# A two-layer attention and MLP kernel: bf16 residual, two-row shift instructions on GpSimd, more plane buffers and another rule table

## The chip, the cores and the metric

The kernel runs on one core of a Trainium2 chip. The metric is the device time of one launch in microseconds; three runs of the kernel before gave 1496.22, 1497.7 and 1498.02 us, a median of 1497.7 us. A profiled execution of the same kernel gives the trace from which all views below come.

The core has five engines with a queue of instructions each: TensorE (PE; its weight loads are shown apart as PEld), VectorE (DVE), ScalarE (ACT), GpSimd (POOL) and SyncE (SP, which only starts DMAs). Each works through its queue in order and waits on semaphores for the others.

## The reference

Two kinds of layer, A and B, are applied in turn, twice, to x of 2048 positions by 512 channels, each on the layer-normed residual stream:

```python
def _A_ref(x, wq, wk, wv, wo):          # H = 32 heads of 16, one key and value head
    q = (x @ wq) split into heads
    k = x @ wk
    v = x @ wv
    scores = einsum("bhqd,bkd->bhqk", q, k) * (Dh ** -0.5)
    p = softmax(scores)
    return (p @ v, heads joined) @ wo

def _B_ref(x, w1, w2, w3, w4):          # w1, w2: 512x512; w3: 512x1792; w4: 1792x512
    h = gelu(layernorm(x) @ w1)
    hs = (four quarters of h, shifted by 1, -1, 2, -2 positions) @ w2
    x1 = x + hs
    return x1 + gelu(layernorm(x1) @ w3) @ w4

x = x + A(layernorm(x)); x = x + B(layernorm(x)); x = x + A(layernorm(x)); x = x + B(layernorm(x))
```

The softmax over 32 x 2048 x 2048 scores, twice, is by far the largest part: 268 million exponentials.

## The kernel before

**Halves.** A layer's attention is worked through in chunks of 512 queries (the last 512 of the second layer as two chunks of 256), each in 8 blocks of four heads, each over 16 tiles of 128 keys. One *half* is one key tile of 512 queries for two of the four heads (at 256 queries two key tiles), so a layer has 1024 halves and the kernel 2048. `make_groups` lists them in order. A half needs two score matmuls (`qk`, L1079), 1024 exponentials in each of 128 partitions, and matmuls P·V (`declare_pv`, L1203) that add into one PSUM bank, ACC, with a 17th column of ones for the softmax denominator.

**Two ways to the exponential.** A half is either a *unit* (`declare_unit`): ScalarE reads two score banks and writes EA (L1123), and one P·V of four matmuls takes it. Or it is a *pair* (`declare_pair`): VectorE turns each score bank into the bit pattern of a bf16 number by one multiply and add into 16-bit integers, the plane J (two instructions of 128x512, L1144). That is a power of two with a straight line between powers, and to lessen its error two copies shifted by 43 and by 85 (a third and two thirds of the 128 steps of an exponent) are made, the planes JK (L1154, 128x1024 each), and P·V runs three times, on J and both JK, with value matrices VD scaled by `PARTS`. The shifts go to GpSimd while fewer than `ADDS` of them are pending there, else to VectorE.

**The rest.** After a block, `block_end` copies ACC, forms reciprocals and normalises. After a chunk, `chunk_end` declares the output projection (L1423 adds it to the residual X), and the MLP: `mixer_in` (layer norm, w1, GELU of GP on ScalarE, L1466), `mix` (w2, L1504), `mlp` (layer norm, w3, evictions G by L1541, GELU of G by L1546), `mlp_out` (w4, L1567 adds to X, or L1572 writes the output), and `next_kv` (layer norm, keys and values of the next layer). GELU and exponential need different ScalarE tables, so each change between them is a table load. The residual X is float32 (X32), with the bf16 input in the upper halves of the same rows (X16).

**The layer boundary.** Halves of the second layer's first chunk need keys of all positions, but their first blocks may run early on the keys that exist: 7 blocks over key tiles 0 to 5, then over tiles 6 to 10 (`EARLY`), with the partial sums spilled to SBUF. So 1024 + 84 = 1108 halves can be done before keys of tiles 6 to 10 are there.

**The order.** `Plan` is a list scheduler that runs when the program is built: it keeps a model of the engines, takes the ready operation of the best priority, and emits a fixed order for each engine. `assign` decides when a half becomes a pair. A table of rules (`MOODS`), chosen anew for each stretch of 12.5 us of planned time by a character of `TEMPER`, sets its thresholds. Where TensorE would be idle, `filler` adds matmuls of zeros (ONES, NIL). Three PSUM banks are shared by pairs and all MLP work; units have four of their own in two slots.

Of the kernel before, what the change touches and what calls it, by code (L numbers as in the profile page):

```python
# [8 lines left out]
dt = mybir.dt  # L9
# [6 lines left out]
class Late:  # L16


    __slots__ = ("bank", "ops", "gates")

    def __init__(self):
        self.bank = None
        self.ops = []
        self.gates = []


class Op:
    __slots__ = ("eng", "emit", "preds", "npend", "succ", "dur", "prio", "seq", "ready", "start",
                 "end", "take", "give", "dma", "out", "pos", "sem", "vc", "side", "placed", "pe", "feeds", "port", "parts", "after", "entry")


class Plan:
# [170 lines left out]
    def _pick(self, eng, t, dense=False):  # L203
# [15 lines left out]
        for o in h:  # L219
            if o.ready > t + 1e-9 or o.entry > t + self.EAGER:  # L220
                continue
            if eng == "ACT" and self.closing and o.side and not all(u.placed for u in self.units[-4:]):
                continue
            if joins and (o.pe[0] != self.pe_kind or self.begin(o, t) > t + 1e-9):
                continue
            if limit and o.prio > 0:
                end = self.run_end(o, t)
                if (not joins or end > self.pe_end + 0.02) and \
                        any(end + (self.SWITCH if o.pe[0] != "Q" else 0.0) > x for x in limit):
                    continue  # L230
            if pressing and self.run_end(o, t) > self.pe_end + 0.02:
                continue
            key = (low.get(o, o.prio), o.seq)
            if self.CLOSE and eng == "PE" and o.prio > 2 and o not in low and o.take is None:
                key = (self.CLOSE, o.seq)
            if stick and o.prio > 2 and o.pe[0] == self.pe_kind and not any(self.run_end(o, t) + self.SWITCH > x for x in due):
                key = (self.STICK, o.seq)
            if o in pinned:
                key = (self.PINNED, o.seq)
            if best is not None and key > best[0]:  # L240
                continue
            k = None
            if o.take is not None:
                if not all(p.placed and (p.end <= t + 1e-9 or p.eng == "PE") for p in o.take.gates):
                    continue
                margin = self.MARGIN if o.side else self.LAT["PE"]
                for i, (ft, b) in enumerate(self.pool):
                    if ft + margin <= t + 1e-9 and (k is None or ft < self.pool[k][0]):
                        k = i
                if k is None or o.prio > 2 and len(self.pool) <= self.SPARE and self.attach is not None and not self.loose:  # L250
                    continue
            best = (key, o)
            bank = k
# [4 lines left out]
        if o.take is not None:  # L258
            b = self.pool.pop(bank)[1]
            o.take.bank = b  # L260
            last = self.pool_last.get(b)
            if last is not None:
                o.preds.add(last)
# [63 lines left out]
    def _place(self, o, t):  # L327
# [51 lines left out]
        if o.give is not None:  # L379
            self.pool.append((o.end, o.give.bank))  # L380
            self.pool_last[o.give.bank] = o
            heapq.heappush(self.events, o.end + self.LAT["PE"])
            heapq.heappush(self.events, o.end + self.MARGIN)
# [146 lines left out]
class Kernel:  # L530
# [12 lines left out]
    N_EA = 6  # L543
    N_J = 4
    N_JK = 5
    STEPS = (0, 43, 85)
    ADDS = 4
    PARTS = (0.3203125, 0.25390625, 0.2021484375)
# [8 lines left out]
    AHEAD = 2  # L557
    MAX_PAIRS = 2
# [27 lines left out]
    TEMPER = "0004c7ec07f77e4f907027ef07eeee79fc406e0770e7473e37722cc100f0b580559f773c3777120e4e54ee2fe471e1217c7e4070c38e21c731"  # L586
# [25 lines left out]
    def memory(self):  # L612
        self.sbytes = 0
        sb = self.sb
        x32 = self.stack.enter_context(self.nc.sbuf_tensor("X32", [128, 16 * 512], dt.float32))[:, :]
        self.sbytes += 32768
        self.X32 = self.shaped(x32, [16, 512])
        self.X16 = self.shaped(x32.bitcast(dt.bfloat16), [16, 1024])[:, :, 512:1024]
# [27 lines left out]
        self.J = sb("J", [self.N_J, 1024], dt.uint16)  # L646
        self.JK = sb("JK", [self.N_JK, 1024], dt.uint16)
        spare = self.JK[:, 0, :].bitcast(dt.bfloat16)
        self.G2E = [(self.EA[:, f // 2, f % 2, :], ("EA", f // 2)) for f in range(2 * self.N_EA)]
        self.G2E += [(spare[:, f * 512:(f + 1) * 512], ("JK", 0)) for f in range(14 - 2 * self.N_EA)]  # L650
# [59 lines left out]
    def head(self):  # L710
# [9 lines left out]
        def load_x(c):  # L720
            for h in range(2):
                t0 = c * 4 + h * 2
                load(self.X16[:, t0:t0 + 2, :], xin[:, t0:t0 + 2, :],
                     [("X", t0), ("X", t0 + 1)], 2 * 131072, c)
# [161 lines left out]
    def ln_in(self, la, tiles, prio=None):  # L886
# [3 lines left out]
        src = (lambda tb: self.X16[:, tb, :]) if la == 0 else (lambda tb: self.X32[:, tb, :])  # L890
        base = (self.QS, "QS") if la and tiles[0] > 2 else (self.ZR, "ZR")
        slot = self.slot(la, c)
        for part in self.portions(tiles):
            self.stats(src, part, lambda tb: ("X", tb), prio)
            self.rstd(part, prio)
            for tb in part:
                self.apply(base[0][:, tb % 4, :], src(tb), tb, [("X", tb)], [(base[1], tb % 4)],
                           0.456 if la else 0.355, prio)
# [120 lines left out]
    def make_groups(self):  # L1019
# [25 lines left out]
        for g in gs:  # L1045
            if g[5]:
                self.segs.append(dict(at=g[0:3], end=None, left=0, held=[], open=False))
            seg = self.segs[-1]
            seg["end"] = g[6]
            for p in range(2):  # L1050
                seg["left"] += 1
                self.halves.append(g[0:5] + (p, len(self.segs) - 1, g[5]))
        self.hi = 0
# [6 lines left out]
        self.waiting = []  # L1060
        self.nfill = 0
# [67 lines left out]
    def declare_pair(self, g):  # L1129

# [4 lines left out]
        js = m % self.N_J  # L1137
        J = self.J[:, js, :]
        for i in range(2):
# [5 lines left out]
                out=J[:, i * 512:(i + 1) * 512], in0=self.PB[:, L.bank, :],  # L1145
                scalar1=128 * LOG2E * 0.25, scalar2=float(127 * 128), op0=ALU.mult, op1=ALU.add),
                writes=[L, ("J", js, i)], dur=t_ps(512), prio=1, side=False, give=L)
        jt = [("J", js, 0), ("J", js, 1)]
        es = [(J, jt)]
        for k in (1, 2):  # L1150
            r = (2 * m + k - 1) % self.N_JK
            self.adds = [p for p in self.adds if not p.placed]
            eng = "POOL" if len(self.adds) < self.ADDS else "DVE"
            x = op(eng, lambda e, k=k, r=r: e.tensor_scalar(  # L1154
                out=self.JK[:, r, :], in0=J, scalar1=float(self.STEPS[k]), scalar2=1.0, op0=ALU.add,
                op1=ALU.mult),
               reads=jt, writes=[("JK", r)], dur=t_x4(1024) if eng == "DVE" else 1.12, prio=2, side=False, port=True,
                   after=0.0 if eng == "DVE" else 0.07)
            if eng == "DVE":
                o = x  # L1160
            else:
                self.adds.append(x)
            es.append((self.JK[:, r, :], [("JK", r)]))
        self.pairs.append(o)
        self.add_pv(g, [(self.shaped(ap.bitcast(dt.bfloat16), [2, 512]), tg, k, m) for k, (ap, tg) in enumerate(es)])

    def add_pv(self, g, es):
        self.segs[g[6]]["held"].append((g, es))
        while True:
            seg = self.segs[self.seg]  # L1170
            held, seg["held"] = seg["held"], []
            for g, es in held:
                if es[0][2] is None or seg["open"]:
                    for x in es:
                        self.declare_pv(seg, g, *x[:3])
                    seg["left"] -= 1
                    if es[0][2] is not None:
                        self.waiting.remove(es[0][3])
                else:
                    seg["held"].append((g, es))  # L1180
# [164 lines left out]
    def assign(self, now, p):  # L1345
# [12 lines left out]
        if self.pl.backlog() > y or \  # L1358
                self.waiting and self.ndve - self.waiting[0] >= min(self.N_J, self.N_JK // 2):
            return False  # L1360
        d = self.hi + self.AHEAD
        while d < len(self.halves) and (self.halves[d][7] or self.halves[d][5] != p or d in self.given):
            d += 1
# [46 lines left out]
    def outproj(self, la, tb, prio=4):  # L1410
# [3 lines left out]
        for h in range(2):  # L1414
            def fpe(e, h=h):
                ins = None
                for b in (2 * h, 2 * h + 1):
# [4 lines left out]
        res = self.X16 if la == 0 else self.X32  # L1422
        op("DVE", lambda e: e.tensor_tensor(out=self.X32[:, tb, :], in0=self.PB[:, L.bank, :],  # L1423
                                            in1=res[:, tb, :], op=ALU.add),
           writes=[L, ("X", tb)], dur=t_ps(512), give=L, prio=prio)

    def mixer_in(self, la, c, tiles, tail):
# [4 lines left out]
        for part in self.portions(tiles):  # L1432
            self.stats(lambda tb: self.X32[:, tb, :], part, lambda tb: ("X", tb), None)
            self.rstd(part, None, both=True)
            for tb in part:
                self.apply(self.Y[:, tb % 6, :], self.X32[:, tb, :], tb, [("X", tb)], [("Y", tb % 6)], 0.456, None)
# [71 lines left out]
    def mlp(self, la, tiles, tail):  # L1508
# [12 lines left out]
        for tb in tiles:  # L1521
            op("POOL", lambda e, tb=tb: e.tensor_tensor(out=self.X32[:, tb, :], in0=self.Y[:, tb % 6, :],  # L1522
                                                       in1=self.X32[:, tb, :], op=ALU.add),
# [28 lines left out]
    def mlp_out(self, la, tiles, tail=False):  # L1552
        op = self.pl.op
        G = [x[0] for x in self.G2E] if tail else [self.G2[:, f, :] for f in range(14)]
        for i, tb in enumerate(tiles):
# [10 lines left out]
            if la == 0:  # L1566
                op("DVE", lambda e, tb=tb, L=L: e.tensor_tensor(  # L1567
                    out=self.X32[:, tb, :], in0=self.PB[:, L.bank, :], in1=self.X32[:, tb, :], op=ALU.add),
                   writes=[L, ("X", tb)], dur=t_ps(512), give=L)
            else:  # L1570
                ob = tb % 2
                op("DVE", lambda e, tb=tb, L=L, ob=ob: e.tensor_tensor(  # L1572
                    out=self.OUTB[:, ob, :], in0=self.PB[:, L.bank, :], in1=self.X32[:, tb, :], op=ALU.add),
# [39 lines left out]
```

The softmax here doesn't subtract the row's maximum and nothing guards it: scores larger than these inputs give would overflow.

## Time and profile before

| | |
|---|---|
| median of three runs | 1497.7 us |
| the profiled execution's span | 1495.4 us |
| exponentials on ScalarE (units) | 1433 |
| pairs on VectorE | 615 |
| shifts on GpSimd / on VectorE | 1014 / 216 |
| table loads on ScalarE | 28 |
| mean granted TensorE clock | 1.000 |

In the profile a group's row names line, engine, operation, output and inputs, then count, busy time, mean duration and the idle time ahead of it with what ended most of it. Durations of one engine can overlap: a mean of 1132 ns with 1433 of them in 1318.8 us of busy time means that a new one starts every 0.920 us. The busy time by stretches, in us from the span's start (columns: stretch, length, then busy time and count of PE, PEld, DVE, ACT, POOL, then clock, DMA share and GB/s):

```profile
0.00:736.00 736.00, 722.26 (x13517) 301.95 (x13521) 687.70 (x1223) 724.85 (x774) 630.92 (x663) 1.00 0.08 19
736.00:834.00 98.00, 96.46 (x1964) 45.91 (x1960) 68.81 (x140) 85.78 (x84) 44.49 (x53) 1.00 0.01 3
834.00:1434.00 600.00, 590.99 (x13295) 268.44 (x13290) 545.90 (x958) 599.50 (x640) 524.19 (x538) 1.00 0.04 10
1434.00:1496.00 62.00, 58.57 (x1388) 36.17 (x1380) 30.55 (x66) 19.50 (x27) 12.96 (x23) 1.00 0.07 22
```

The first stretch is the head and layer one, the second the boundary between the layers, the third layer two, the last the MLP of the last queries.

### The profile page before, as it was taken

How to read it: one execution, taken by the hardware profiler on the slowest of the kernel's cores; microseconds unless marked ns; L12 is line 12 of the kernel's file. 1: busy time of each engine (PE TensorE's matmuls, PEld its weight loads, DVE VectorE, ACT ScalarE, POOL GpSimd, SP SyncE). 2: the span in 40 equal slices, each digit the busy share in tenths (PEclk: the TensorE clock that was granted, in tenths of full speed). 3: DMA queues.
4: the chain of work that ended last, by engine and by line, in shares of the span. 5: the costliest groups of instructions: out<-in, count | busy, mean ns of one | idle time of the engine just before them, and what ended most of it. 6: DMA issues, size and time to landing. Idle time of an engine off the chain costs nothing.

```text
span 1495.4 us, 66501 instructions
## 1 busy us (share of the span) xinstructions
PE 1468.3 (98%) x30149; PEld 652.5 (44%) x30149; DVE 1332.9 (89%) x2385; ACT 1429.6 (96%) x1521; POOL 1212.6 (81%) x1275
## 2 busy tenths in 40 slices
PE   9999999999999999999999999999999999999999
PEld 4443434444343444443444444444443344555555
DVE  8999999989999999998786799999989999988973
ACT  7999999999999999999979999999999999999962
POOL 2999999878899888889744698899878999788951
DMA  6100100001000000010000000010000000000000
GB/s 214 30 5 6 20 6 6 4 7 20 6 6 5 6 6 5 6 19 2 2 3 3 3 8 11 5 20 6 9 19 8 5 6 7 12 19 11 7 14 24
DMA packets 32155, 21.72 MB, mean 15 GB/s; under 512 B 12672, under 2 KB 31360, under 8 KB 31872
## 3 DMA queue, kind: packets, MB, share of 16 engines
q1 hardware_dynamic: 31872, 17.47, 4.9%
q8 instruction: 235, 3.85, 1.0%
q14 instruction: 48, 0.39, 0.1%
HBM read 7.90 MB, written 2.10 MB: 7 GB/s over the span
## 4 chain that ended last, share of the span: by engine, by line
ACT 62%; PE 30%; DVE 5%; POOL 2%; issue 1%; DMA 0%
ACT EA L1123 59%; PE PB L676 10%; PE PB L1079 9%; PE PB L1203 9%; DVE J L1144 2%; POOL JK L1154 2%; ACT G L1546 1%; DVE ST L791 1%; ACT L1123 1%; PE PB L875 1%; DVE G L1541 1%; ACT GP L1466 1%; PE PB L932 0%; DVE X L1423 0%; POOL ZR L1437 0%
## 5 line engine op out<-in xcount | busy, mean ns | idle before, releaser
L1123 ACT ACTIVATE EA<-PB 128x1024 bf16<-128x1024 f32 x1433 | 1318.8, 1132 | 9.4 <-PE PB L1079 7.8
L1154 POOL TENSOR_SCALAR JK<-J 128x1024 uint16<-128x1024 uint16 x1014 | 1075.9, 1061 | 156.2 <-DVE J L1144 66.7
L1144 DVE TENSOR_SCALAR J<-PB 128x512 uint16<-128x512 f32 x1230 | 789.0, 679 | 65.6 <-PE PB L1079 61.0
L1079 PE MATMUL PB<-QT,KT 32*128 32x512 bf16 (+1 forms) x4608 | 610.8, 360 | 13.3 <-ACT EA L1123 6.6
L1203 PE MATMUL PB<-EA,VP 128*32 128x256 bf16 (+1 forms) x6460 | 366.4, 263 | 0.5 <-DVE ACCF L1237 0.3
L1079 PEld LDWEIGHTS PB<-QT,KT 32*128 32x128 bf16 x4608 | 164.4, 91 | 372.0 <-ACT EA L1123 279.9
L1203 PE MATMUL PB<-JK,VD 128*32 128x256 bf16 (+1 forms) x5512 | 321.4, 266 | 4.6 <-POOL JK L1154 2.6
L1203 PEld LDWEIGHTS PB<-EA,VP 128*32 128x32 bf16 x6460 | 154.3, 95 | 114.3 <-issue 88.3
L1203 PEld LDWEIGHTS PB<-JK,VD 128*32 128x32 bf16 x5512 | 126.6, 94 | 163.4 <-issue 86.0
L1203 PE MATMUL PB<-J,VD 128*32 128x256 bf16 (+1 forms) x2756 | 174.1, 264 | 0.3 <-DVE J L1144 0.2
L676 PE MATMUL PB<-ZT,W 128*32 128x512 bf16 (+2 forms) x2816 | 168.0, 342 | 0.6 <-DVE ZT L884 0.3
L1154 DVE TENSOR_SCALAR JK<-J 128x1024 uint16<-128x1024 uint16 x216 | 152.1, 712 | 2.5 <-PE PB L1203 1.1
L676 PE MATMUL PB<-W,G 128*32 128x512 bf16 x1624 | 104.6, 380 | 0.3 <-DVE J L1144 0.2
L1203 PEld LDWEIGHTS PB<-J,VD 128*32 128x32 bf16 x2756 | 67.6, 95 | 44.6 <-issue 36.2
L1541 DVE CAST G<-PB 128x512 bf16<-128x512 f32 (+2 forms) x126 | 71.8, 579 | 14.0 <-PE PB L676 12.8
L676 PEld LDWEIGHTS PB<-ZT,W 128*32 128x32 bf16 x2816 | 64.1, 96 | 33.8 <-issue 18.6
L1546 ACT ACTIVATE G<-G 128x1792 bf16<-128x1792 bf16 x29 | 47.0, 1686 | 24.5 <-DVE G L1541 24.4
L811 POOL TENSOR_TENSOR SM<-SM,MH 128x2 f32<-128x2 f32 (+1 forms) x69 | 49.4, 717 | 22.4 <-DVE SM L813 16.3
L676 PE MATMUL PB<-ONES,NIL 128*32 128x512 bf16 x612 | 56.4, 398 | 1.7 <-DVE YT L884 1.0
L676 PEld LDWEIGHTS PB<-W,G 128*32 128x32 bf16 x1624 | 38.0, 96 | 36.3 <-issue 10.7
L1268 DVE TENSOR_TENSOR OS<-ACCF,PB 128x512 bf16<-128x512 bf16 (+1 forms) x72 | 44.5, 618 | 3.7 <-PE PB L1262 3.2
L1522 POOL TENSOR_TENSOR X<-Y,X 128x512 f32<-128x512 bf16 x32 | 37.3, 1169 | 11.7 <-DVE Y L1504 10.0
(108 smaller groups left out, 845.9 us busy)
## 6 DMA issues: line engine op xcount, KB each, us to landing
OT<-OS SPq DMA_DIRECT2D x424, 8.0 KB, 1.8
W<-in_B_w_dram SPq DMA_DIRECT2D x2, 1792.0 KB, 14.7
X<-in_A_x_dram SPq DMA_DIRECT2D x8, 256.0 KB, 5.2
QT<-QS SPq DMA_DIRECT2D x32, 64.0 KB, 2.5
out_dram<-OUTB SPq DMA_DIRECT2D x16, 128.0 KB, 1.8
OT<-OS SPq DMA_DIRECT2D x104, 4.0 KB, 1.8
W<-in_B_w_dram SPq DMA_DIRECT2D x2, 512.0 KB, 8.9
WQ<-in_A_wq_dram SPq DMA_DIRECT2D x1, 512.0 KB, 4.9
```

The lines of the kernel that those rows point to most:

```text
L676: ins = e.matmul(self.PB[32 * g:32 * g + 32, bank, 0:n], lhsT=lhsT[:, 32 * g:32 * g + 32], rhs=rhs, start=start, stop=stop, tile_position= ...
L791: op("DVE", lambda e, tb=tb: e.bn_stats(self.ST6[:, tb, :], src(tb)), reads=[tagf(tb)], writes=[("ST", tb)], dur=0.606, prio=prio)
L811: op("POOL", lambda e: e.tensor_tensor(out=out, in0=src, in1=self.MH[:, 0, a:b], op=ALU.pow), reads=tags + [("MH",)], writes=tg(r), dur=0. ...
L1079: ins = e.matmul(self.PB[:, bank, j * n:(j + 1) * n], lhsT=self.KT[32 * h:32 * h + 32, la, (kb + j) * 128:(kb + j + 1) * 128], rhs=self.QT ...
L1123: o = q.feeds = op("ACT", lambda e: e.activation(self.EA[:, ea, :, :], self.PB[:, b0:b0 + 2, :], ACTF.Exp, scale=0.25), writes=bk + [("EA" ...
L1144: o = op("DVE", lambda e, i=i, L=L: e.tensor_scalar(out=J[:, i * 512:(i + 1) * 512], in0=self.PB[:, L.bank, :], scalar1=128 * LOG2E * 0.25 ...
L1154: x = op(eng, lambda e, k=k, r=r: e.tensor_scalar(out=self.JK[:, r, :], in0=J, scalar1=float(self.STEPS[k]), scalar2=1.0, op0=ALU.add, op1 ...
L1203: ins = e.matmul(self.PB[32 * x:32 * x + 32, self.ACC, p * hw:p * hw + hw], lhsT=v[:, la, kb + j, :], rhs=ap[:, i, j * w + u * hw:j * w + ...
L1268: op("DVE", lambda e: e.tensor_tensor(out=osm, in0=acc, in1=self.PB[:, M.bank, 0:n], op=ALU.mult), reads=am, writes=[M] + om, dur=t_ps(n), ...
L1522: op("POOL", lambda e, tb=tb: e.tensor_tensor(out=self.X32[:, tb, :], in0=self.Y[:, tb % 6, :], in1=self.X32[:, tb, :], op=ALU.add), reads ...
L1541: op("DVE", lambda e, f=f, L=L: e.tensor_copy(self.G2[:, f, 0:n], self.PB[:, L.bank, 0:n]), writes=[L] + [(x, f, i) for x in ("G2", "GE") ...
L1546: op("ACT", lambda e, i=i: e.activation(self.G2[:, :, i * 128:(i + 1) * 128], self.G2[:, :, i * 128:(i + 1) * 128], ACTF.Gelu_apprx_tanh), ...
```

## The change

Four things are changed together.

1. The residual is one bf16 array X; X32 and X16 go. All additions to it, statistics and normalisations read and write bf16.
2. The planes of a pair are three rows of one array J, in one of `N_J` = 5 slots. The second row is the first plus 43, the third the second plus 43 (86 in all, where it was 85; `PARTS` follows). One instruction (`shift_op`) makes the second row of this pair and the third row of the pair before, by a slice with a stride: 128x2x1024. So the third P·V of a pair is declared with the next pair, and the last pair of a block gets its third row by a single-row instruction (`finish_pair`). The limit `ADDS` counts rows.
3. EA has 8 buffers in place of 6, and J 15 rows where J and JK had 4 and 5.
4. `TEMPER` is another string, so the scheduler comes to another order everywhere.

Beside these, a bank can be taken several at a time (`Late.n`), which nothing uses, and `MARGIN_END` is 0, which changes nothing.

```diff
-    N_EA = 6
-    N_J = 4
-    N_JK = 5
-    STEPS = (0, 43, 85)
+    N_EA = 8
+    N_J = 5
+    STEP = 43
-    PARTS = (0.3203125, 0.25390625, 0.2021484375)
+    PARTS = (0.3203125, 0.25390625, 0.201171875)
-    TEMPER = "0004c7ec07f77e4f907027ef07eeee79fc406e0770e7473e37722cc100f0b580559f773c3777120e4e54ee2fe471e1217c7e4070c38e21c731"
+    TEMPER = "090ee27f7f97f71e3eee4ee77f547c4fe941e77e7385715f85317197105502005897e0e10e0ef77f27f593f70f1f030e1e77ee0975325855000003"
...
-        x32 = self.stack.enter_context(self.nc.sbuf_tensor("X32", [128, 16 * 512], dt.float32))[:, :]
-        self.X32 = self.shaped(x32, [16, 512])
-        self.X16 = self.shaped(x32.bitcast(dt.bfloat16), [16, 1024])[:, :, 512:1024]
+        self.X = sb("X", [16, 512])
...
-        self.J = sb("J", [self.N_J, 1024], dt.uint16)
-        self.JK = sb("JK", [self.N_JK, 1024], dt.uint16)
+        self.J = sb("J", [3 * self.N_J, 1024], dt.uint16)
...
-        jt = [("J", js, 0), ("J", js, 1)]
-        es = [(J, jt)]
-        for k in (1, 2):
-            r = (2 * m + k - 1) % self.N_JK
-            self.adds = [p for p in self.adds if not p.placed]
-            eng = "POOL" if len(self.adds) < self.ADDS else "DVE"
-            x = op(eng, lambda e, k=k, r=r: e.tensor_scalar(
-                out=self.JK[:, r, :], in0=J, scalar1=float(self.STEPS[k]), scalar2=1.0, op0=ALU.add,
-                op1=ALU.mult),
-               reads=jt, writes=[("JK", r)], dur=t_x4(1024) if eng == "DVE" else 1.12, prio=2, side=False, port=True,
-                   after=0.0 if eng == "DVE" else 0.07)
...
+        last, self.later = self.later, (g, m)
+        self.shift([m] if last is None else [last[1], m])
+        self.add_pv(g, [self.term(m, 0), self.term(m, 1)], m, 0)
+        if last is not None:
+            self.add_pv(last[0], [self.term(last[1], 2)], last[1], 1)
...
+    def shift(self, ms):
+
+        rows = sorted(3 * (m % self.N_J) + (2 if len(ms) == 2 and m == ms[0] else 1) for m in ms)
+        n = len(rows)
+        d = slice(rows[0], rows[-1] + 1, rows[-1] - rows[0] if n > 1 else 1)
+        f = slice(rows[0] - 1, rows[-1], rows[-1] - rows[0] if n > 1 else 1)
+        self.shift_op(d, f, rows)
+
+    def finish_pair(self):
+
+        (g, m), self.later = self.later, None
+        r = 3 * (m % self.N_J) + 2
+        self.shift_op(slice(r, r + 1), slice(r - 1, r), [r])
+        self.add_pv(g, [self.term(m, 2)], m, 1)
+
+    def shift_op(self, d, f, rows):
+        n = len(rows)
+        self.adds = [p for p in self.adds if not p.placed]
+        eng = "POOL" if sum(p.weight for p in self.adds) < self.ADDS else "DVE"
+        o = self.pl.op(eng, lambda e: e.tensor_scalar(
+            out=self.J[:, d, :], in0=self.J[:, f, :], scalar1=float(self.STEP), scalar2=1.0, op0=ALU.add, op1=ALU.mult),
+            reads=[t for r in rows for t in self.jtag(r - 1)], writes=[t for r in rows for t in self.jtag(r)],
+            dur=t_x4(1024 * n) if eng == "DVE" else 0.27 + 0.853 * n, prio=2, side=False, port=True,
+            after=0.0 if eng == "DVE" else 0.07)
+        if eng == "DVE":
+            self.pairs[-1] = o
+        else:
+            o.weight = n
+            self.adds.append(o)
...
-                self.waiting and self.ndve - self.waiting[0] >= min(self.N_J, self.N_JK // 2):
+                self.waiting and self.ndve - self.waiting[0] >= self.N_J:
...
-        res = self.X16 if la == 0 else self.X32
-        op("DVE", lambda e: e.tensor_tensor(out=self.X32[:, tb, :], in0=self.PB[:, L.bank, :],
-                                            in1=res[:, tb, :], op=ALU.add),
+        op("DVE", lambda e: e.tensor_tensor(out=self.X[:, tb, :], in0=self.PB[:, L.bank, :],
+                                            in1=self.X[:, tb, :], op=ALU.add),
```

## The prediction

> **What bounds the kernel now.** I read the engine table first, then the groups, then ScalarE's own timeline and waits, then the end on TensorE, and last the order of instructions on each engine in both programs. The first fence has lines of the engine table, the chain, the groups (count, busy us and mean ns, idle us ahead of them) and the waits (us in total, times, longest).
>
> ```profile
> PE 1468.3 (98%) x30149; PEld 652.5 (44%) x30149; DVE 1332.9 (89%) x2385; ACT 1429.6 (96%) x1521; POOL 1212.6 (81%) x1275
> ACT 62%; PE 30%; DVE 5%; POOL 2%; issue 1%; DMA 0%
> L1123 ACT ACTIVATE EA<-PB 128x1024 bf16<-128x1024 f32 x1433 | 1318.8, 1132 | 9.4 <-PE PB L1079 7.8
> L1154 POOL TENSOR_SCALAR JK<-J 128x1024 uint16<-128x1024 uint16 x1014 | 1075.9, 1061 | 156.2 <-DVE J L1144 66.7
> L1144 DVE TENSOR_SCALAR J<-PB 128x512 uint16<-128x512 f32 x1230 | 789.0, 679 | 65.6 <-PE PB L1079 61.0
> L1154 DVE TENSOR_SCALAR JK<-J 128x1024 uint16<-128x1024 uint16 x216 | 152.1, 712 | 2.5 <-PE PB L1203 1.1
> PEld PB L1079 <- ACT EA L1123: 279.9, 955, 1.1
> PEld PB L1203 <- POOL JK L1154: 56.7, 219, 0.8
> ```
>
> TensorE is shown busier than ScalarE, but its weight loads for scores (L1079) wait 279.9 us for ScalarE to free a score bank, so its busy share contains queueing. ScalarE holds 62% of the chain. It is the bound while attention runs, and its pitch is 1318.8/1433 = 0.920 us for one exponential (the mean of 1132 ns overlaps the next one).
>
> Where ScalarE is not full is the question. By windows it is idle 11.2 us in 0 to 736, 12.2 us in 736 to 834, 0.5 us in 834 to 1434, and 42.5 us in the last 62. Its timeline at the layer boundary and at the end:
>
> ```profile
> 744.64 1.89 ACT L1466 ACTIVATE GP<-GP 128x2048 bf16<-128x2048 bf16 x1
> 746.56 1.28 ACT L1123 ACT_TABLE_LOAD   x1
> 747.85 1.94 ACT L1123 ACTIVATE EA<-PB 128x1024 bf16<-128x1024 f32 x2
> 752.11 24.89 ACT L1123 ACTIVATE EA<-PB 128x1024 bf16<-128x1024 f32 x27 [2.32 <-PE PB L1079]
> 777.01 1.28 ACT L1546 ACT_TABLE_LOAD   x1
> 786.58 4.87 ACT L1546 ACTIVATE G<-G 128x1792 bf16<-128x1792 bf16 x3 [8.28 <-DVE G L1541]
> ...
> 1434.09 1.28 ACT L1466 ACT_TABLE_LOAD   x1
> ```
>
> At the boundary there are no scores to exponentiate: ScalarE waits 2.32 and 8.28 us, then (same view) 0.42 and 1.03, together 12.05. The last exponential ends at 1434.09, and 61.3 us of MLP follow. That end is TensorE's; its first part:
>
> ```profile
> 1434.54 0.28 PE L1203 MATMUL PB<-EA,VP 128*32 128x128 bf16 x8
> 1434.65 1.90 PE L676 MATMUL PB<-ZT,W 128*32 128x512 bf16 x32
> 1436.37 0.20 PE L1247 MATMUL PB<-SELC,ACCF 128*32 128x4 bf16 x8
> 1436.43 1.47 PE L676 MATMUL PB<-ZT,W 128*32 128x512 bf16 x24
> ...
> 1440.85 2.01 PE L676 MATMUL PB<-WO,OT 128*32 128x512 bf16 x32
> ```
>
> The reader sees the last block's normalisation (L1247 and on) standing behind earlier MLP matmuls: 6.3 us from the last P·V at 1434.54 to the output projection at 1440.85.
>
> **What the Trainium skill says.** "ScalarE: Activation LUTs", section "What ACT_TABLE_LOAD costs", gives 1283 ns for a load plus about 1380 ns of drain. The trace has 1283 exactly, but no drain: after the load at 746.56 the exponential starts at 747.85. I price a switch at 1.283 us and keep 2.66 as the upper end. "SBUF — State Buffer", section "SBUF: two separate sides", says that GpSimd and a VectorE operation in a two-port mode take the shared ports as an exclusive lock for a whole instruction. The trace agrees: the same shift on VectorE takes 361 ns at least and 1293 at most, a spread of 0.93 us beside GpSimd instructions of 1.06. "GPSIMD Engine Reference", section "Elementwise — side-by-side cycle accounting", puts about 156 ns of dispatch on each instruction; the smallest GpSimd operation here (L817, 128x2) takes 233 ns, which contains it.
>
> **The change, part by part.** Both programs have a fixed order, so I count. The new rule table issues nothing itself; what it does is in these counts and places.
>
> ScalarE. There are 1419 exponentials for 1433: 14 x 0.920 = 12.9 us less. Exponential and GELU alternate more often: 31 table loads for 27 stand ahead of the last exponential, +4 x 1.283 = +5.1 us (+10.6 with the skill's drain). The 256-wide GP GELU (1.06 us), now behind the last exponential, moves ahead of it: +1.1. Sum -6.7 us with every wait unchanged.
>
> The boundary. In the old order TensorE reaches 1112 halves (half = 128 keys x 512 queries x two heads) and then runs over 300 matmuls of MLP, transposes and K projection without one score matmul between them: the second group of early keys needs the MLP of chunk 2, whose W4 matmuls end only there. In the new order these end at 1069 halves and the K projection at 1089, ahead of the 1108 halves that the first group allows; scores then run all through the W3 and W4 matmuls. Between the output projection of layer 0 and the end of its MLP stand 133 halves instead of 110. The work of TensorE in that stretch hardly moves: 168 W4 matmuls x 0.065 and 64 W1 x 0.074 leave it (-15.6), 46 score matmuls x 0.162 and 164 P·V x 0.065 come (+18.2). ScalarE has 41 exponentials in place of 29 between GP and the next G, 37.7 us and two loads, where 42 us pass now from GP's start to G: just covered. So up to 12.05 us of waiting goes; I take 9, since the last G evictions of layer 0 end now (826.6) only 2.4 us ahead of the GELU that reads them, and that chain is late next.
>
> The end. Behind the last score matmul stand 80 fewer real matmuls (48 of W1/W3 kind, 32 of GP), 8 more fillers and 8 more P·V: about -80 x 0.065 + 0.7 + 0.3 = -4.2 us if TensorE sets it. From the last P·V to the output projection the chain of small VectorE and TensorE steps takes its place, so I count -2.5 (0 to -4.2).
>
> GpSimd. 1014 instructions of 1.061 us become 494 of two rows and 62 of one. A two-row instruction isn't in the trace. Lower end: a whole 233 ns saved, 2 x 1.061 - 0.233 = 1.89; with the skill's dispatch saved, 1.97 (estimate); nothing saved, 2.12. I take 1.9: 494 x 1.9 + 62 x 1.06 = 1004, 72 less. All of that is beside ScalarE's work and counts nothing by itself. If it is longer than the order was made for (0.27 + 0.853 x 2 in the diff, about 1.9 after its end allowance), TensorE, which takes its matmuls in order, waits at a P·V with all score matmuls queued behind.
>
> VectorE. 28 more J conversions x 0.641 = +18. Shifts: 216 x 0.704 become 101 two-row and 6 single ones. A two-row body lies between 0.36 and 0.72; I take 0.63, plus a wait that grows with GpSimd's instruction (0.704 - 0.361 = 0.34 now, x 1.9/1.06 = 0.61): 101 x 1.24 + 6 x 1.0 = 131, -21. Some 80 normalisations also wait about 0.27 longer, +21; 48 of them read bf16 for f32, -0.1 each (0.50 against 0.40 in the undisturbed end), -5. Sum +13 us, 1346 of some 1480, 91%: no relief, but 134 us of slack against 162.
>
> The buffers (EA 8 for 6, J 5 slots) cover the later third term of each pair; it is now made with the next pair, and 62 blocks end with a single shift of 1.06 us that the accumulator copy waits for. ScalarE has waited for a P·V once in all (1.03 us), so I cost it at nothing; without the cover it would be 62 times up to about 1 us. TensorE's P·V: 180 more of J, 60 fewer of EA, 80 fewer fillers: 120 x 0.065 - 80 x 0.092 = +0.4 us, nothing. Residual stores and statistics keep their lengths (f32 677 ns, bf16 671 at L791).
>
> Sum: -6.7 - 9 - 2.5 = -18.2 us from the span of 1495.4, 1477.2. The median of the runs stands 2.3 above the span: 1479.5. I say 1480.
>
> **The rivals.**
> 1. Counts alone: the waits at the boundary only move (to the second G of layer 0, or behind the new loads). For it: that chain had 2.4 us to spare. Against: scores are available all along in the new order. -6.7 - 2.5 gives 1488.5.
> 2. Slower: the two-row GpSimd instruction. If it saves no overhead (2.12 us), each result comes some 0.2 us late in stretches where GpSimd is at 90%, and TensorE stops ahead of the score matmuls. It decides from 18.2/494 = 37 ns per instruction reaching ScalarE; 60 ns would give 1497.7 - 18.2 + 29.6 = 1509. For it: 219 such waits stand in the profile already, and no two-row instruction does. Against: these 56.7 us reach ScalarE as only 7.8 us, and the fixed share of 233 ns.
> 3. No change: half of that lateness (37 ns), or VectorE's longer waits for the port holding banks, eats the gain: about 1498.
>
> **How the numbers follow.** Main case 0.62 (its own range 1471 to 1488), rival 1 0.20 (1485 to 1494), rival 2 0.11, rival 3 0.07. Full removal of the waits with the whole 4.2 at the end is 1474.8; a few us of unseen gain reach 1471. The upper end takes in rival 1 with the skill's drain (+5.5 on 1488.5). Range 1471 to 1494. 0.2%, 3 us, is what can be told from no change here: faster 0.83, same 0.06, slower 0.11.
>
> **What would show it.** Right: no wait over 3 us on ScalarE between 736 and 834; the last exponential near 1418; TensorE still waiting for ScalarE some 280 us at L1079's successor; two-row GpSimd near 1.9 us. Rival 1 shows as a G GELU waiting for VectorE; rival 2 as weight loads of P·V waiting for GpSimd well over 57 us and ScalarE's waits for scores well over 8. The prediction is wrong if ScalarE's exponentials get gaps in 0 to 736 or 834 to 1418, where it had almost none.

## The result, and the profile after

The changed kernel takes 1482.72 us (median of 4 runs, 1481.02 to 1483.94) against 1497.7 before: a ratio of 0.9896, interval 0.9882 to 0.991. The profiled execution's span is 1479.2 us against 1495.4, 16.2 us less.

The engine table and the costliest groups of the changed kernel (busy us, share, instructions; then count, busy us and mean ns, idle us ahead and what ended most of it):

```profile
PE 1454.1 (98%) x30189; PEld 651.1 (44%) x30189; DVE 1285.0 (87%) x2304; ACT 1421.3 (96%) x1511; POOL 1146.2 (77%) x817
...
ACT 74%; PE 21%; DVE 3%; POOL 1%; issue 0%; DMA 0%; POOLq 0%
...
L1125 ACT ACTIVATE EA<-PB 128x1024 bf16<-128x1024 f32 x1419 | 1305.2, 1169 | 11.3 <-PE PB L1081 5.3
...
L1143 DVE TENSOR_SCALAR J<-PB 128x512 uint16<-128x512 f32 x1258 | 808.5, 682 | 84.3 <-PE PB L1081 79.0
```

The two forms of the shift, from the groups with shapes kept apart:

```profile
L1180 POOL TENSOR_SCALAR J<-J 128x2048 uint16<-128x2048 uint16 x494 | 939.5, 1902 | 212.7 <-DVE J L1143 113.8 <-DVE J L1180 63.2 <-DVE MV L793 3.0
L1180 DVE TENSOR_SCALAR J<-J 128x2048 uint16<-128x2048 uint16 x101 | 73.2, 724 | 8.5 <-POOL J L1180 7.8
```

The two-row shift takes 1.902 us on GpSimd, where two single ones took 2 x 1.061. ScalarE holds more of the chain than before, 74% for 62%. That share alone doesn't tell what bounds the kernel: the kernel before with only its residual in bf16, first of the runs below, has 80% and is 1.4 us faster. Waits of TensorE's weight loads, of GpSimd and of the exponentials (us in total, times, longest):

```profile
PEld PB L1081 <- ACT EA L1125: 316.6, 1083, 0.8
...
POOL J L1180 <- DVE J L1180: 66.2, 57, 3.1
...
PEld PB L1230 <- POOL J L1180: 19.8, 72, 0.7
...
ACT EA L1125 <- PE PB L1230: 5.3, 4, 2.4
```

TensorE waits less for GpSimd (19.8 us for 56.7) and more for ScalarE (316.6 for 279.9). ScalarE's timeline at the layer boundary:

```profile
749.07 1.91 ACT L1493 ACTIVATE GP<-GP 128x2048 bf16<-128x2048 bf16 x1
751.01 1.28 ACT L1125 ACT_TABLE_LOAD   x1
752.30 13.86 ACT L1125 ACTIVATE EA<-PB 128x1024 bf16<-128x1024 f32 x15
767.52 23.94 ACT L1125 ACTIVATE EA<-PB 128x1024 bf16<-128x1024 f32 x26 [1.37 <-PE PB L1230]
791.48 1.28 ACT L1573 ACT_TABLE_LOAD   x1
792.77 4.87 ACT L1573 ACTIVATE G<-G 128x1792 bf16<-128x1792 bf16 x3
...
815.25 7.44 ACT L1125 ACTIVATE EA<-PB 128x1024 bf16<-128x1024 f32 x8 [2.44 <-PE PB L1230]
823.41 3.77 ACT L1125 ACTIVATE EA<-PB 128x1024 bf16<-128x1024 f32 x4 [0.72 <-PE PB L1230]
...
1384.33 36.25 ACT L1125 ACTIVATE EA<-PB 128x1024 bf16<-128x1024 f32 x39
1420.59 1.28 ACT L1573 ACT_TABLE_LOAD   x1
```

The G GELU at 792.77 starts right behind its table load; the 8.28 us in front of it are gone, because exponentials fill the time. What is left are three waits for a P·V, 4.53 us together. In the stretches 0 to 736 and 834 to the last exponential, which ends at 1420.58, ScalarE is idle for 12.4 and 0.6 us, about as before (11.2 and 0.5). At the end, on TensorE:

```profile
1420.93 0.29 PE L1230 MATMUL PB<-EA,VP 128*32 128x128 bf16 x8
1421.04 0.29 PE L1230 MATMUL PB<-J,VD 128*32 128x128 bf16 x8
...
1424.35 0.38 PE L676 MATMUL PB<-ONES,NIL 128*32 128x512 bf16 x2
1425.29 1.91 PE L676 MATMUL PB<-WO,OT 128*32 128x512 bf16 x32 [0.56 <-DVE OT L1314]
```

From the last P·V to the output projection 4.25 us pass for 6.3, and now TensorE waits for that chain of small steps, fillers and all.

The 16.2 us of span, added up from these views:

| term | us |
|---|---|
| 14 exponentials fewer, 0.920 each | -12.9 |
| 4 table loads more ahead of the last exponential, 1.283 each | +5.1 |
| the 256-wide GP GELU moved ahead of it | +1.1 |
| ScalarE's waits at the boundary, 12.05 to 4.53 | -7.5 |
| the exponentials' other waits for TensorE, 5.1 to 6.1 | +1.0 |
| last exponential to the end, 61.3 to 58.6 | -2.7 |
| sum (measured -16.2) | -15.9 |

This is an account of one engine's time. TensorE's busy time falls by nearly as much (1468.3 to 1454.1), so the sum doesn't show that ScalarE alone holds the kernel; the runs with shorter exponentials below bear on that.

### The profile page after: what moved, and what is told of

The parts are those of the page before. It is cut to its first block, busy times and chain, and to the rows that moved or that the text cites. A ratio compares the mean times of both kernels' runs of the same rounds, so it can differ in the third digit from the quotient of the medians.

```text
span 1479.2 us, 66152 instructions
## 1 busy us (share of the span) xinstructions
PE 1454.1 (98%) x30189; PEld 651.1 (44%) x30189; DVE 1285.0 (87%) x2304; ACT 1421.3 (96%) x1511; POOL 1146.2 (77%) x817
## 4 chain that ended last, share of the span: by engine, by line
ACT 74%; PE 21%; DVE 3%; POOL 1%; issue 0%; DMA 0%; POOLq 0%
ACT EA L1125 69%; PE PB L676 7%; PE PB L1081 7%; PE PB L1230 6%; ACT G L1573 3%; ACT L1125 1%; DVE J L1143 1%; ACT GP L1493 1%; POOL J L1180 1%; ACT L1573 1%; ACT L1493 1%; PE PB L875 1%; DVE ST L791 0%; DVE G L1568 0%; PE PB L932 0%
## 5 line engine op out<-in xcount | busy, mean ns | idle before, releaser
L1125 ACT ACTIVATE EA<-PB 128x1024 bf16<-128x1024 f32 x1419 | 1305.2, 1169 | 11.3 <-PE PB L1081 5.3
L1180 POOL TENSOR_SCALAR J<-J 128x2048 uint16<-128x2048 uint16 (+1 forms) x556 | 1006.1, 1810 | 233.5 <-DVE J L1143 126.4
L1143 DVE TENSOR_SCALAR J<-PB 128x512 uint16<-128x512 f32 x1258 | 808.5, 682 | 84.3 <-PE PB L1081 79.0
L1230 PE MATMUL PB<-J,VD 128*32 128x256 bf16 (+1 forms) x8448 | 413.9, 265 | 2.1 <-POOL J L1180 0.8
L1230 PE MATMUL PB<-EA,VP 128*32 128x256 bf16 (+1 forms) x6400 | 350.8, 263 | 0.7 <-DVE KT L1242 0.4
L1081 PEld LDWEIGHTS PB<-QT,KT 32*128 32x128 bf16 x4608 | 162.7, 91 | 385.0 <-ACT EA L1125 316.6
L1230 PEld LDWEIGHTS PB<-J,VD 128*32 128x32 bf16 x8448 | 176.1, 95 | 176.0 <-issue 133.9
L1180 DVE TENSOR_SCALAR J<-J 128x2048 uint16<-128x2048 uint16 (+1 forms) x107 | 78.9, 737 | 8.8 <-POOL J L1180 7.9
L791 DVE BATCH_NORM_STATS2 ST<-X 128x6 f32<-128x512 bf16 x64 | 43.1, 681 | 1.8 <-DMA X<-in_A_x_dram 1.3
L1549 POOL TENSOR_TENSOR X<-Y,X 128x512 bf16<-128x512 bf16 x32 | 38.6, 1218 | 6.3 <-DVE Y L1531 4.6
L1264 DVE CAST ACCF<-PB 128x512 bf16<-128x512 f32 (+1 forms) x65 | 40.0, 615 | 2.5 <-PE PB L1230 2.4
```

The costliest lines, as they stand in the source:

```text
L791: op("DVE", lambda e, tb=tb: e.bn_stats(self.ST6[:, tb, :], src(tb)), reads=[tagf(tb)], writes=[("ST", tb)], dur=0.606, prio=prio)
L1081: ins = e.matmul(self.PB[:, bank, j * n:(j + 1) * n], lhsT=self.KT[32 * h:32 * h + 32, la, (kb + j) * 128:(kb + j + 1) * 128], rhs=self.QT ...
L1125: o = q.feeds = op("ACT", lambda e: e.activation(self.EA[:, ea, :, :], self.PB[:, b0:b0 + 2, :], ACTF.Exp, scale=0.25), writes=bk + [("EA" ...
L1143: o = op("DVE", lambda e, i=i, L=L: e.tensor_scalar(out=self.J[:, 3 * s, i * 512:(i + 1) * 512], in0=self.PB[:, L.bank, :], scalar1=128 * ...
L1180: o = self.pl.op(eng, lambda e: e.tensor_scalar(out=self.J[:, d, :], in0=self.J[:, f, :], scalar1=float(self.STEP), scalar2=1.0, op0=ALU.a ...
L1230: ins = e.matmul(self.PB[32 * x:32 * x + 32, self.ACC, p * hw:p * hw + hw], lhsT=v[:, la, kb + j, :], rhs=ap[:, i, j * w + u * hw:j * w + ...
```

## The experiments

All ratios are against the kernel before, run beside each. Where an engine's order is said to be kept, only what an instruction issues was changed, not what the planner was told of it. Differences from the changed kernel compare medians of different runs (the kernel before had medians of 1497.3 to 1498.2 beside them), so those of about 1 us mean nothing.

**The bf16 residual by itself.** The kernel before, order kept:

```diff
-        x32 = self.stack.enter_context(self.nc.sbuf_tensor("X32", [128, 16 * 512], dt.float32))[:, :]
-        self.sbytes += 32768
-        self.X32 = self.shaped(x32, [16, 512])
-        self.X16 = self.shaped(x32.bitcast(dt.bfloat16), [16, 1024])[:, :, 512:1024]
+        self.X32 = self.X16 = sb("X", [16, 512])
```

> The kernel before with every engine's order kept and only the residual in bf16 (one array in place of float32 and its bf16 halves). Theory (the bf16 residual as such moves nothing on the path; it only makes room for the buffers): within 0.2% of the kernel before, 1495 to 1500 us, with normalisations of the residual at some 0.1 us less each and ScalarE's exponentials and table loads the same in number. Rival (its shorter VectorE operations are part of the gain): 3 us or more faster.

1495.87 us, ratio 0.999 (0.9982 to 0.9998). The normalisation Y<-X falls from 681 to 531 ns. So bf16 by itself gives 1.4 us, 2.7 at the end of the interval, and the rival is out. Its 16 KB of each partition make room for the buffers.

**A dearer shift, order kept.** First two one-row instructions for each two-row one on GpSimd:

```diff
-        o = self.pl.op(eng, lambda e: e.tensor_scalar(
-            out=self.J[:, d, :], in0=self.J[:, f, :], scalar1=float(self.STEP), scalar2=1.0, op0=ALU.add, op1=ALU.mult),
+        cuts = [(d, f)] if eng == "DVE" else [(slice(r, r + 1), slice(r - 1, r)) for r in rows]
+        o = self.pl.op(eng, lambda e: [e.tensor_scalar(
+            out=self.J[:, x, :], in0=self.J[:, y, :], scalar1=float(self.STEP), scalar2=1.0, op0=ALU.add, op1=ALU.mult)
+            for x, y in cuts][-1],
```

> The changed kernel with every engine's order kept, but each two-row shift on GpSimd is issued as two one-row instructions, so the overhead that the two-row form saves is paid again: 494 x (2 x 1.06 - 1.90) = 108 us more of GpSimd, 77% to about 85% of the span. Theory (GpSimd's time is beside ScalarE's work and not on the path): TensorE's waits for GpSimd grow from 20 us to some 60, the time rises by 1 to 10 us and stays below the kernel before. Rival (the cheaper shift is what made the kernel faster): the gain goes back, +13 us or more, to 1495 or above.

1564.75 us, ratio 1.0449 (1.0435 to 1.0463): 82 us more than the changed kernel, where my theory had 1 to 10. Engine table and waits of this run:

```profile
PE 1480.2 (95%) x30189; PEld 648.3 (41%) x30189; DVE 1291.5 (83%) x2304; ACT 1451.3 (93%) x1511; POOL 1240.6 (79%) x1311
```

```profile
PEld PB L1081 <- ACT EA L1125: 168.9, 555, 0.8
PEld PB L1232 <- POOL J L1181: 140.6, 281, 1.5
...
PE PB L1232 <- POOL J L1181: 57.2, 138, 1.3
...
ACT EA L1125 <- PE PB L1081: 53.2, 139, 2.1
```

GpSimd's busy time grew by 94.4 us and the time by 82, 0.87 us for each (the toll in what follows), although GpSimd is idle for a fifth of the span. The P·V matmuls and their weight loads now wait 198 us for GpSimd, with score matmuls queued behind them, and ScalarE, which waited 5 us for scores, waits 53. VectorE's busy time hardly moves (1285.0 to 1291.5), so slower VectorE instructions aren't the reason.

Then three instructions (1024, 512 and 512 columns) in the same place:

```diff
+        cuts = [(d, f, slice(0, 1024))] if n == 1 or eng == "DVE" else [
+            (slice(r, r + 1), slice(r - 1, r), slice(u, u + w))
+            for r, u, w in ((rows[0], 0, 1024), (rows[1], 0, 512), (rows[1], 512, 512))]
```

> As the run with two one-row instructions, but three (1024, 512 and 512 columns), about 2.46 us by the group means of 1061 ns for 1024 and 697 ns for 512 elements: 277 us more of GpSimd, about 95% of the span. Theory: here GpSimd's results come late enough to stop TensorE ahead of score matmuls, and the time rises steeply, by 30 to 120 us; the step from the first split to this one is far larger than the step to the first. Rival (GpSimd was the bound already): the rise is proportional to the added time from the first 0.22 us on, about 2.5 times that of the first split.

1678.97 us, ratio 1.1213 (1.1198 to 1.1229): +196 us for 190.7 us more of GpSimd (1336.9). The rise is near to proportional from the start, as the rival had it, 0.87 us for each us in the first step and 1.19 in the second; there is no stretch that costs little before a steep one. (The mean granted clock was 0.976 here and 0.999 in the changed kernel; how much of the 196 us belongs to that wasn't separated.)

**The same toll on the kernel before.** 413 of its 1014 GpSimd shifts as two halves, order kept:

```diff
+            cuts = [slice(0, 512), slice(512, 1024)] if eng == "POOL" and k == 2 else [slice(0, 1024)]
             x = op(eng, lambda e, k=k, r=r, cuts=cuts: [e.tensor_scalar(
-                out=self.JK[:, r, :], in0=J, scalar1=float(self.STEPS[k]), scalar2=1.0, op0=ALU.add,
-                op1=ALU.mult),
+                out=self.JK[:, r, z], in0=J[:, z], scalar1=float(self.STEPS[k]), scalar2=1.0, op0=ALU.add,
+                op1=ALU.mult) for z in cuts][-1],
```

> The kernel before with every engine's order kept, but 413 of its 1014 GpSimd shifts (the second of a pair) issued as two instructions of 512 columns, 2 x 0.618 us in place of 1.06 by the run with three instructions: about 72 us more of GpSimd. New theory (in an order laid out this tightly a late GpSimd result stops TensorE, whichever kernel it is, since all score matmuls stand behind the P.V that waits): the same toll as in the changed kernel, 0.87 us per us added, so some +63 us, near 1560. Rival (only the changed kernel is so tight, because its shifts are a chain of two-row instructions each of which reads what the last one wrote): less than half of it, below 1530.

1581.52 us, ratio 1.0556 (1.054 to 1.0572): +83 us for 81.8 us more of GpSimd (1294.4 for 1212.6), above the 63 expected: 1.02 us for each us. The toll is no property of the chained two-row form; both kernels have it.

**A cheaper shift, order kept.** Does the toll run the other way?

```diff
+        w = 1024 if n == 1 or eng == "DVE" or self.ndve < 16 else 768
-            out=self.J[:, d, :], in0=self.J[:, f, :], scalar1=float(self.STEP), scalar2=1.0, op0=ALU.add, op1=ALU.mult),
+            out=self.J[:, d, 0:w], in0=self.J[:, f, 0:w], scalar1=float(self.STEP), scalar2=1.0, op0=ALU.add, op1=ALU.mult),
```

> The changed kernel with every engine's order kept; from the 16th pair on the two-row shifts on GpSimd cover 768 of 1024 columns, so a quarter of the second and third terms is what stood there before. About 0.4 us less for each of some 480, 200 us less of GpSimd in all. Theory (ScalarE is full; a faster GpSimd has nothing to give): 1475 to 1483 us, the gain at most the 10 us that ScalarE now waits for scores and free buffers. Rival (GpSimd is the bound, so that time goes with it both ways): 1400 or less.

1481.66 us, ratio 0.9887 (0.9871 to 0.9904), 1 us from the changed kernel and within the noise (its runs lie between 1481.02 and 1483.94):

```profile
PE 1452.6 (98%) x30189; PEld 650.5 (44%) x30189; DVE 1276.0 (86%) x2304; ACT 1421.6 (96%) x1511; POOL 936.7 (63%) x817
```

GpSimd is 209.5 us less busy, and ScalarE's line is the same as in the changed kernel (1421.3). The rival, that GpSimd's time goes with the kernel's both ways, is out: in this order a later result costs at once and an earlier one gives nothing.

**A cheaper exponential, order kept.** 960 of 1024 columns, in the changed kernel, then with the short shifts, then in the kernel before:

```diff
+        w = 512 if k < 16 else 480
-        o = q.feeds = op("ACT", lambda e: e.activation(self.EA[:, ea, :, :], self.PB[:, b0:b0 + 2, :], ACTF.Exp,
+        o = q.feeds = op("ACT", lambda e: e.activation(self.EA[:, ea, :, 0:w], self.PB[:, b0:b0 + 2, 0:w], ACTF.Exp,
```

> The changed kernel with every engine's order kept; from the 17th unit on an exponential covers 960 of its 1024 columns, so a sixteenth of those terms is what stood there before. 64 columns at (1686 - 920)/(1792 - 1024) = 1.0 ns by the profile's GELU and exponential are 60 us or so less of ScalarE. Theory (ScalarE is the bound, with GpSimd's chain close behind, since adding to that one cost at once): the time falls, but by 10 to 40 us only, and weight loads of P.V wait for GpSimd well over 20 us. Rival (ScalarE alone binds): it falls by all of the 60 us. Second rival (GpSimd and TensorE bind, ScalarE only looks full): it falls by less than 5.

1472.41 us, ratio 0.9831 (0.9816 to 0.9846): 10.3 us less, at the low edge of what I expected. The 60 us of the expectation are themselves too small: back to back, an exponential starts 0.850 us after the one before it where it was 0.904, and 54 ns for 1403 of them are some 76 us (estimate from the two traces). Chain and waits of this run:

```profile
PE 75%; DVE 12%; POOL 7%; ACT 5%; issue 1%; DMA 0%; POOLq 0%
...
PEld PB L1081 <- issue: 166.6, 713, 0.6
PEld PB L1081 <- ACT EA L1126: 134.3, 392, 0.8
...
PEld PB L1231 <- POOL J L1181: 38.2, 129, 0.7
```

TensorE waits for ScalarE 134 us for 317, and 167 us of its idle time ahead of score matmuls now end with no wait that the profile shows ("issue"). The chain is mostly TensorE's own work.

> Short exponentials (960 columns) and short two-row GpSimd shifts (768 columns) together, order kept, both leaving those columns as they were. Theory (two bounds side by side): the fall is clearly larger than the sum of the two alone (short shifts alone gave 1 us), 40 to 60 us below the changed kernel. Rival (TensorE or VectorE is the next bound, not GpSimd): no more than the short exponentials alone.

1461.08 us, ratio 0.9758 (0.9744 to 0.9773): 21.6 us less than the changed kernel, where the two alone gave 10.3 and 1.1. That is more than their sum, so GpSimd's chain does stand next to ScalarE; but it is half of the 40 to 60 expected, and most of the 76 us still doesn't show. P·V loads wait only 6.8 us for GpSimd here. What holds the rest is TensorE by the chain of this run:

```profile
PE 80%; DVE 10%; ACT 9%; issue 0%; DMA 0%; SPq 0%
```

No run made TensorE's work shorter, so this last step is read from the chain and not shown.

> The kernel before with the short exponentials (960 of 1024 columns), order kept. Theory: as in the changed kernel, the time falls by part of the 60 us, 10 to 40, since its GpSimd is as close behind (81% busy, the same toll for added time). Rival (before had ScalarE alone as its bound, and the change brought GpSimd up to it): it falls by twice as much as the changed kernel does, or more.

1493.15 us, ratio 0.9975 (0.9964 to 0.9986): only 4.4 us. I had the sign and not the size; the rival (twice the changed kernel's fall) is out. With the exponentials shortened, the P·V loads of the kernel before wait for GpSimd twice as long as the 38.2 us of the changed one:

```profile
PEld PB L1204 <- POOL JK L1155: 79.1, 296, 0.9
```

By the second rival's measure in the run on the changed kernel (a fall of less than 5 us where ScalarE only looks full), ScalarE alone did not hold the kernel before, though its timeline between 834 and 1434 has 0.5 us of idle time. As I read these runs, ScalarE, GpSimd's chain and TensorE stood side by side there, with less than half of the room that the changed kernel has behind ScalarE.

**Structure and rule table.** Only the string TEMPER was changed here: each structure with the other's table, and both with the single character "0", the first row of the rules for all stretches.

> The changed kernel with the rule table of the kernel before. Theory (the gain is in the order that the table picks, and a table fits only the structure it was found for): slower than both kernels, by 20 us or more over 1483, with more exponentials left on ScalarE (1440 by its order against 1419) and longer waits of ScalarE for scores. Rival (the two-row shift, the buffers and the bf16 residual carry the gain, the table a detail): 1475 to 1490 us.

1562.79 us, ratio 1.0434 (1.0385 to 1.0483). The 1440 exponentials are there, and they wait 36.4 us for TensorE where the changed kernel's wait 10.6.

> The kernel before with the rule table of the changed one. Theory (a table fits only its structure): slower than 1498 by 20 us or more; its order has 1457 exponentials on ScalarE for 1433. Rival (the new table is better in general and alone makes the gain): 1480 to 1490 us.

1552.26 us, ratio 1.0364 (1.0334 to 1.0394). The 1457 exponentials are there, and they wait 42.3 us for TensorE where the kernel before has 8.8.

> The changed kernel with one rule for all stretches (the first row of the rules, no table). Its order leaves 1468 exponentials on ScalarE. Theory (without a table fitted to it the new structure brings nothing): within 1% of the kernel before with the same single rule, and both well above 1498. Rival (the structure carries the gain of 1%): 10 us or more faster than that.

1538.14 us, ratio 1.0269 (1.024 to 1.0299).

> The kernel before with one rule for all stretches; its order leaves 1471 exponentials on ScalarE for 1433. It is the other half of the comparison without tables: 38 exponentials more are 35 us if nothing else moves, so 1520 to 1545. Theory: within 1% of the changed kernel with the same single rule. Rival: 10 us or more slower than it.

1534.78 us, ratio 1.0247 (1.0217 to 1.0277).

| | table of before | table of after | one rule |
|---|---|---|---|
| structure of before | 1497.7 | 1552.3 | 1534.8 |
| structure of after | 1562.8 | 1482.7 | 1538.1 |

Against a single rule, its own table gains the old structure 37 us and the new one 55, and the other's table costs 17 and 25. With the single rule the new structure is no faster (3.4 us slower, intervals overlap). ScalarE has 1468 exponentials there in the new structure and 1471 in the old, 49 and 38 more than with their tables; at 0.920 us these are 45 of the 55 us and 35 of the 37. So the 15 us between the two kernels are the difference of two fitted orders. How much of it the new structure allows that the old one couldn't have with a longer search isn't settled by these runs: they hold two fitted tables, one for each structure. Nor does any run have the buffers or the two-row shift by itself.

## Why the prediction was right

- **ScalarE's counts** (-6.7): measured -12.9, +5.1 and +1.1. Loads took 1.283 us each, with no drain behind them (the load at 751.01, the exponential at 752.30), and the exponential's pitch stayed 0.920. Exact, as counts of a fixed order can be.
- **ScalarE as the bound** ("It is the bound while attention runs"): too simple. With some 76 us taken off its exponentials, the kernel before gains 4.4 us. As I read it, 14 exponentials fewer were worth their 12.9 us because the new order relieved the others too: P·V loads wait 19.8 us for GpSimd instead of 56.7. No run takes the 14 out by themselves.
- **The boundary** (-9 of 12.05): -7.5. The mechanism is as told: scores run through W3 and W4, and the G GELU no longer waits. The term was 1.5 us too large because the larger EA pool didn't cover every late P·V. The step that ScalarE "has waited for a P·V once in all (1.03 us), so I cost it at nothing" is short by 4.3 us: 5.3 us in four waits for 1.03 in one. In the trace each of these four P·V begins within 0.3 us of the end of VectorE's copy of a finished block's accumulator (L1242, L1248 and L1264). So what came late is the end of a block, in 4 of the 62 where the prediction set a cost without the cover; only two of the four have a single-row shift in the 4 us ahead of them.
- **The end** (-2.5): -2.7, and TensorE waits there for the chain of small steps, as said.
- **Two-row shifts on GpSimd** (1.9 us, "counts nothing by itself"): 1.902 us, and the run with shorter shifts shows that less still gives nothing. More costs at once: the saving that the two-row form brings is one that this order can't do without, 82 us by the run with two one-row instructions. The figure was hit partly by luck. The floor of 1.89 took 233 ns as the whole of the smallest GpSimd operation, but the same trace has memsets of 0.10 us; the saving by the runs is about 0.19 us.
- **VectorE** (+13 us busy): wrong. It fell by 48, from 1332.9 to 1285.0. The step that failed is the port wait: I scaled it with GpSimd's longer instruction and put 1.24 us on a two-row shift. It takes 0.724 on average, and 92 of the 101 in the trace take 0.63 to 0.70. Most two-row shifts read a row that the shift before them wrote, so one on VectorE and one on GpSimd seldom run side by side; GpSimd waits instead, 66.2 us in 57 waits for VectorE's shift, in the view of waits above. In the trace 209 of the 216 VectorE shifts of the kernel before overlap a GpSimd instruction, and 33 of the 101 now; all nine above 0.70 us began while a GpSimd instruction ran, one of them a shift. The 101 shifts alone are 52 us of the miss (101 x 0.52). The normalisations were to take 16 us more; the 64 at L828 take 38.3 us for 40.1. It cost nothing that the sum shows, with VectorE at 3% of the chain, and rival 3's longer port waits didn't come.
- **Rival 2** (a dearer two-row shift): its mechanism holds. 82 us for 494 instructions is 166 ns each reaching ScalarE, of some 190 added; at that rate 18.2 us would have been gone at about 42 ns added, close to the 37 ns worked out; no run stands that low. Its time of 1509 for no saving at all was far too low, 1564.75 by the run: I let 60 ns of 220 through, on the ground that 56.7 us of waits reached ScalarE as 7.8. That ratio belongs to waits which the order had been laid out with; for added ones it is nearly one to one.
- **Rival 1** would have shown as a G GELU waiting for VectorE; neither of the two at the boundary waits, and the longest wait of ScalarE between 736 and 834 is 2.44 us. The last exponential ends at 1420.58 where 1418 was said.

The sum was 2 us too favourable in the span, 1477.2 for 1479.2: 1.5 at the boundary and 1.0 in other waits, less 0.2 that the end gave.

## What to carry to other kernels

When a scheduler fixes the order of every engine, count the bound engine's instructions and look where its waits are in the old trace, then see in the new order whether something else stands in those places: four counts and one gap gave this result within 3 us. A full timeline doesn't make an engine the only bound: shorten its work with the order kept and see how much of it the time follows, here 4.4 of 76 us before and 10.3 after. An engine with a fifth of its time idle may still have no slack: ask what stands behind the instruction that waits for it, and test it by making that work dearer and cheaper with the order kept. Don't compare two structures with a table that was fitted to one of them.

## What the runs showed of the hardware that wasn't expected

- GpSimd's shift of 1024 elements takes 1.047 us by the run with two one-row instructions, 512 take 0.618, 1536 in two rows 1.476 and 2048 in two rows 1.902: about 0.19 us and 0.84 ns for each element, and a second row with a stride between adds no fixed cost that shows.
- A VectorE shift of 2048 16-bit elements in two rows takes 0.68 us in most cases, undisturbed; the shortest of 1024 took 0.36.
- How long VectorE's normalisations stand beside GpSimd depends on the order more than on the length of GpSimd's instructions: ZR<-Y takes 606 ns on average in the kernel before and 574 in the changed one, with instructions of 1.06 and 1.90 us, but 789 and 891 in the same structures with the single rule, where GpSimd is no busier (77% and 73%). In the changed kernel's order it takes 458 with the short shifts and 574 with the whole ones, but 641 and 632 where two or three shorter instructions stand for each whole one, so there too it doesn't follow the length.
